# Nyström attention and a multiplicative feed-forward on one Trainium2 core: the landmark product on GpSimd, the norm chain as a stage of its own, and the stages interleaved from a written list

## The chip, the cores and the metric

The kernel runs on one core of a Trainium2 chip. The metric is device time in microseconds; lower is better. A core has five engines that run side by side, each taking its own instructions in program order: TensorE (PE in the profile; its weight loads are PEld), VectorE (DVE), ScalarE (ACT), GpSimd (POOL) and SyncE (SP), which here only issues transfers. Matmuls write PSUM; VectorE and ScalarE read it.

## The reference, cut to what matters

Each of 8 batch items ("images" below) has 8 heads of 576 rows of 64 numbers. Attention goes through 32 landmarks, means of 18 rows each. The result of all heads, 4608 rows of 512, goes through the feed-forward.

```python
q_lm = q.reshape(B, H, m, S // m, D).mean(axis=3)      # m = 32
k_lm = k.reshape(B, H, m, S // m, D).mean(axis=3)
A  = softmax(q @ k_lm.T / 8)       # 576 x 32
Bm = softmax(q_lm @ k_lm.T / 8)    # 32 x 32
C  = softmax(q_lm @ k.T / 8)       # 32 x 576
Z = Bm.T / (norm1(Bm) * norminf(Bm) + 1e-06)
for _ in range(6):
    Z = 2 * Z - Z @ Bm @ Z
attn = A @ Z @ C @ v
h = (x @ w1) * (x @ w2) @ w3       # x: attn, heads side by side
out = h @ w_out
```

## The kernel before, in words

**Preparation.** `fold` multiplies w3 by w_out once into one matrix `w34`, while the first transfers arrive (L497 to L500). It is a generator: each `steps(fd, n)` lets it emit n more products, and the attention of image 0 is emitted between them. Loads of q and k go through POOL's queue (`qk_pieces`, L93), transposes of them, v and the output through SP's (L106, L85, L467).

**Per image.** `sums` (POOL, L176 to L181) adds rows towards the landmarks, `landmarks` finishes them with a copy on ACT (`far`, L195) and an addition on POOL (L196), into `qbd` and `lm`. Then `attention(st)`, also a generator, emits the small attention products in 13 stages, each ended by `yield`:

1. C0: scores of half the heads against all keys (L211), exponential on ACT into `ect` (L215), partial sums on POOL (`presum`, L222 to L227).
2. B: the landmark scores (L238), `ebm` on ACT (L242), row sums and reciprocal on DVE (`rbs`, L245, L246), the product `bm` on DVE (L248), its 32x32 transpose `bt` (L251), and `btm` on POOL (L253).
3. C1 (the other half of the heads), its presum, then the norm chain on DVE: column sums `cs`, transpose `csT`, maximum, scaling and reciprocal into `nrn` (L261 to L268); `bmn` and `bmbd` on POOL (L270, L273).
4. R: bt times btm (L300), from which DVE makes `sz_` and `tz_`, two operations for each half (L306, L308); then A0 and A1 (L285, exponentials at L291), and cv, C times v (L317), with reciprocal and scaling on DVE (L325, L326).
5. to 10. the six iterations (L376; L381, L383), with denominators (L337), their reciprocals in three parts (L346), and in the last one the first `normalise` (L361, L364).
11. Z (L398), `zt`, the second `normalise`.
12. and 13. G: zt times w1 and w2 (L419), copied to `gt` by ACT (L423) and DVE (L425).

**The main loop** goes over images b. It emits for image b the `up` products (L433): for j in 0 to 7 the half u (w1), copied by ACT to `a_sb` (L437), and the half v (w2), multiplied with a_sb by DVE into `ab` (L439). Then come the `down` products (L451), in halves of four matmuls, 8 halves for an even image and 10 for an odd one, evicted by ACT (L460). Between these it emits the stages of the attention of image b+1, at fixed places: stages 1 to 4 after u1, u2, u4 and u6, stage 5 after v7, and then one stage after each half of down. Here too stand the preparations for image b+2: `sums` after v5, `landmarks` and the four pieces of v. The last image has no attention beside it.

**What sets the order.** The schedule is manual: each engine executes in the order in which the code emits. PSUM has three buffers named `big`, shared by C, A, up, the iterations, normalise, G and part of down; one `acc` (B, R, the second cv, down) and one `small`. A matmul that takes a buffer waits until the engine that reads its last content has done so.

Of the kernel before, what the change touches and what calls it, by code (L numbers as in the profile page):

```python
# [7 lines left out]
FP32 = mybir.dt.float32  # L8
FP16 = mybir.dt.float16
AXF = mybir.ActivationFunctionType  # L10
ALU = mybir.AluOpType
AX = mybir.AxisListType

B = 8
# [17 lines left out]
def kernel(  # L32
# [20 lines left out]
    def big():  # L53
        return psp.tile([128, 2, 512], FP32, name="big", bufs=3)
# [145 lines left out]
    def attention(st, bank=None):  # L200
# [35 lines left out]
        for qd in range(2):  # L236
            for h in range(4):
# [7 lines left out]
        nc.vector.reduce_sum(out=rbs, in_=ebm, axis=AX.X)  # L245
        nc.vector.reciprocal(out=rbs, in_=rbs)  # L246
        bm = pz.tile([128, 2, 32], FP32, name="bm")
        nc.vector.tensor_tensor(out=bm, in0=ebm,  # L248
                                in1=rbs.unsqueeze(2).to_broadcast([128, 2, 32]), op=ALU.mult)
        bt = pz.tile([128, 2, 32], FP32, name="bt")  # L250
        nc.vector.transpose(out=bt, in_=bm)  # L251
        btm = pz.tile([128, 2, 2, 32], FP32, name="btm")
        nc.gpsimd.tensor_tensor(  # L253
            out=btm, in0=bt.unsqueeze(2).to_broadcast([128, 2, 2, 32]),
            in1=par32.unsqueeze(1).unsqueeze(3).to_broadcast([128, 2, 2, 32]), op=ALU.mult)
        yield

        scores_c(1)
        es1 = presum(1)
        cs = pz.tile([128, 2], FP32, name="cs")  # L260
        nc.vector.reduce_sum(out=cs, in_=bt, axis=AX.X)  # L261
        csT = pz.tile([128, 2, 32], FP32, name="csT")
        nc.vector.transpose(out=csT, in_=cs.unsqueeze(2).to_broadcast([128, 2, 32]))
        nrn = pz.tile([128, 2], FP32, name="nrn")
# [28 lines left out]
            eat.append(e)  # L293

        side = acc if bank is acc else (lambda: big()[:, 0, :])
        psR = side()
        for qd in range(2):
            for h in range(4):
# [3 lines left out]
                                 tile_position=(64 * (h // 2), 32 * h))  # L302
        sz_ = pz.tile([128, 2, 96], FP32, name="sz_")
        tz_ = pz.tile([128, 2, 32], FP32, name="tz_")
        for qd in range(2):
            nc.vector.tensor_scalar(out=sz_[:, qd, 0:32], in0=psR[:, 32 * qd:32 * qd + 32],  # L306
                                    scalar1=nrn[:, qd:qd + 1], scalar2=None, op0=ALU.mult)
            nc.vector.scalar_tensor_tensor(  # L308
                out=tz_[:, qd, :], in0=psR[:, 32 * qd:32 * qd + 32], scalar=nrn[:, qd:qd + 1],
                in1=eye2[:, qd, :], op0=ALU.mult, op1=ALU.add)  # L310
        scores_a(0)
        scores_a(1)

        def cv(qd, es, psV):
            for r in range(6):
                for h in range(4):
                    nc.tensor.matmul(  # L317
                        psV[32 * h:32 * h + 32, 0:64], ects[qd][0:NP, h, r, :],
                        vt[0:NP, 4 * qd + h, 64 * r:64 * r + 64],
                        start=(r == 0), stop=(r == 5), tile_position=(0, 32 * h))  # L320
            for h in range(4):
                nc.tensor.matmul(psV[32 * h:32 * h + 32, 64:65], es[0:NP, h, :], ones[0:NP, :],
                                 start=True, stop=True, tile_position=(0, 32 * h))
            rcr = pz.tile([128, 1], FP32, name="rcr")
            nc.vector.reciprocal(out=rcr, in_=psV[:, 64:65])  # L325
            nc.vector.tensor_scalar(out=sz_[:, qd, 32:96], in0=psV[:, 0:64],  # L326
                                    scalar1=rcr[:, 0:1], scalar2=None, op0=ALU.mult)

        psX = small()
        cv(0, es0, psX)  # L330
# [197 lines left out]
    def steps(g, n=1):  # L528
        for _ in range(n):
            next(g, None)  # L530
# [3 lines left out]
    with tc.tile_pool(name="pf", bufs=2) as pf:  # L534
        wof, w3f = {}, {}
        wsp = pf.tile([128, 2, 8, DM], FP16, name="wsp", bufs=1)

        def load_w3(j, cc=None, eng=nc.sync):
            if j not in w3f:
                w3f[j] = pf.tile([128, DF], FP32, name="w3f", bufs=3)  # L540
            sl = slice(0, DF) if cc is None else slice(512 * cc, 512 * cc + 512)
            eng.dma_start(out=w3f[j][:, sl], in_=moe_w3[128 * j:128 * (j + 1), sl])

        def load_wout(c, eng):
            wof[c] = pf.tile([128, DM], FP32, name="wof", bufs=6)
            eng.dma_start(out=wof[c], in_=moe_w_out[128 * c:128 * c + 128, :])

        load_w3(0, 0)
        load_wout(0, nc.scalar)
        load_wout(1, nc.sync)  # L550
        load_w3(1, 0, nc.scalar)
        load_wout(2, nc.sync)
        load_wout(3, nc.scalar)
        load_w3(0, 1)
        load_wout(4, nc.scalar)
        load_w3(1, 1)
        load_wout(5, nc.scalar)

        warm = pf.tile([128, 512], FP16, name="warm", bufs=1)
        nc.vector.memset(warm, 0.0)  # L560
        psw = big()

        def warm_up(n):
            for _ in range(n):
                nc.tensor.matmul(psw[:, 0, :], warm[:, 0:128], warm, start=True, stop=True)

        warm_up(7)

        nc.gpsimd.tensor_copy(out=gate, in_=wof[4][:, 0:1])
        load_qk(sts[0], 0)  # L570
        load_qk(sts[1], 1)
        load_weight(0, moe_w1)
        load_weight(1, moe_w2)
        par32, mask4, ones, eye2, onesq, selc, lomask = constants()
        fd = fold(pf, wof, w3f, wsp, warm_up)
        steps(fd, 1)
        load_wout(6, nc.sync)
        load_wout(7, nc.sync)
        load_w3(2)
        steps(fd, 7)  # L580
        load_w3(3)
        steps(fd, 8)
        w3f[4] = pf.tile([128, DF], FP32, name="w3f", bufs=3)
        nc.gpsimd.tensor_copy(out=w3f[4][0:NP, 0:1], in_=sts[0]["qkn"][0:NP, 0, 0, 0:1])
        load_w3(4)
        sts[0]["vt"] = pin.tile([128, H, 384], FP32, name="vt")
        nc.gpsimd.tensor_copy(out=sts[0]["vt"][0:NP, 0, 0:1], in_=sts[0]["qkn"][0:NP, 1, 0, 0:1])
        load_v(sts[0], 0)
        turn_on_pe(sts[0], 0, 0, nc.scalar.copy)
        turn_on_pe(sts[0], 0, 4, nc.vector.tensor_copy)  # L590
        sums(sts[0], 0)
        steps(fd, 5)
        turn_on_pe(sts[0], 1, 0, nc.scalar.copy)
        turn_on_pe(sts[0], 1, 4, nc.vector.tensor_copy)
        load_w3(5)
        steps(fd, 2)
        landmarks(sts[0], 0, 0)
        landmarks(sts[0], 0, 1)
        sums(sts[0], 1)
        steps(fd, 2)  # L600
        load_w3(6)
        turn_all(1)
        steps(fd, 5)
        at = attention(sts[0])
        for n, m in enumerate((2, 2, 3, 3, 2, 1, 1, 1, 1, 2, 2, 3, 3)):
            steps(at)
            if n == 0:
                load_w3(7)
            elif n == 3:
                pieces = qk_pieces(sts[2], 2)  # L610
                sums(sts[1], 0, pieces=pieces)
                sums(sts[1], 1, pieces=pieces)
            if 2 < n < 7:
                load_v_piece(sts[1], 1, n - 3, ident[0:NP, 0:1])
            elif n > 10:
                landmarks(sts[1], 0, n - 11)
            steps(fd, m)
            if n == 0:
                landmarks(sts[0], 1, 0)
                landmarks(sts[0], 1, 1)  # L620
                steps(fd, 2)
        steps(at, 30)
        landmarks(sts[1], 1, 0)
        steps(fd, 64)
    pab = ctx.enter_context(tc.tile_pool(name="pab", bufs=2))
    at = attention(sts[1], acc)


    for b in range(B):
        st = sts[b]  # L630
        if b % 2 == 0:
            ab = pab.tile([128, 8, 2 * S], FP16, name="ab")
        st["ab"], st["t0"] = ab, S * (b % 2)
        if b + 2 < B:
            turn_all(b + 2)
        chunks = range(0, 512, 128) if b % 2 == 0 else range(512, 2 * S, 128)
        for j in range(8):
            up(st, j, 0)
            if b + 1 < B and j == 0:
                landmarks(sts[b + 1], 1, 1)  # L640
            steps(at, (0, 1, 1, 0, 1, 0, 1, 0)[j])
            if b + 2 < B and j > 5:
                load_v_piece(sts[b + 2], b + 2, j - 6, ident[0:NP, 0:1])
            up(st, j, 1)
            if b + 2 < B and j == 5:
                pieces = qk_pieces(sts[b + 3], b + 3) if b + 3 < B else iter(())
                sums(sts[b + 2], 0, pieces=pieces)
                sums(sts[b + 2], 1, pieces=pieces)
        steps(at, 1)
        hold = {}  # L650
        nd = 2 * len(chunks)
        for n in range(nd):
            bank = (lambda: big()[:, 0, :]) if n // 2 % 2 else acc
            down(ab, b - b % 2, chunks[n // 2], n % 2, hold, bank)
            if b + 2 < B and n in (1, 3):
                load_v_piece(sts[b + 2], b + 2, 2 + n // 2, ident[0:NP, 0:1])
            steps(at)
            if b + 2 < B and n in (3, 4, 6):
                landmarks(sts[b + 2], n // 6, (n == 4) + 0)
        steps(at, 30)  # L660
        if b + 2 < B:
            at = attention(sts[b + 2], acc)
# [30 lines left out]
```

## Time and profile before

| | |
|---|---|
| runs | 280.36 to 283.4 us, median 282.5 us of 5 |
| the profiled execution | 284.0 us, of which 282.2 us from first to last instruction (the span) |
| `up` L433 on PE | 512 matmuls of 128x288 |
| `ab` L439 on DVE | 64, 47.4 us, mean 749 ns |
| `a_sb` L437 on ACT | 64, 40.9 us, mean 639 ns |
| R work on DVE, one image: L306, L308 | 4 operations of about 245 ns |
| `bmn` L270 on POOL, 128x64 | 8, mean 291 ns |
| DMA | 45.57 MB, mean 161 GB/s |

A row gives an engine's work on a line; the mean is that of one instruction, and instructions that overlap in an engine's pipeline stand closer than their means. The granted clock of PE is full throughout.

### The profile page before, as it was taken

How to read it: one execution, taken by the hardware profiler on the slowest of the kernel's cores; microseconds unless marked ns; L12 is line 12 of the kernel's file. 1: busy time of each engine (PE TensorE's matmuls, PEld its weight loads, DVE VectorE, ACT ScalarE, POOL GpSimd, SP SyncE). 2: the span in 40 equal slices, each digit the busy share in tenths (PEclk: the TensorE clock that was granted, in tenths of full speed). 3: DMA queues.
4: the chain of work that ended last, by engine and by line, in shares of the span. 5: the costliest groups of instructions: out<-in, count | busy, mean ns of one | idle time of the engine just before them, and what ended most of it. 6: DMA issues, size and time to landing. Idle time of an engine off the chain costs nothing.

```text
span 282.2 us, 9481 instructions
## 1 busy us (share of the span) xinstructions
PE 265.7 (94%) x3964; PEld 148.1 (52%) x3964; DVE 164.4 (58%) x439; ACT 137.2 (49%) x259; POOL 162.4 (58%) x210
## 2 busy tenths in 40 slices
PE   7999879899999999999999989999999999999993
PEld 3456435344674466447645654566467446734741
DVE  7734134555287576655765756577568755766610
ACT  3644444026461675357537624664386266615531
POOL 1716863297269948964896599259956954400000
PEclk9999999999999999999999999999999999999999
DMA  6999999999906995899699939995999452014024
GB/s 220 313 234 245 213 251 170 153 253 154 167 5 136 240 219 109 138 281 144 137 174 260 177 90 210 203 169 122 218 197 154 125 161 74 2 39 107 9 74 112
DMA packets 61978, 45.57 MB, mean 161 GB/s; under 512 B 35568, under 2 KB 54000, under 8 KB 61936
## 3 DMA queue, kind: packets, MB, share of 16 engines
q1 hardware_dynamic: 47280, 31.93, 49.8%
q0 software_dynamic: 13824, 11.54, 28.5%
q10 hardware_dynamic: 832, 1.51, 1.6%
q8 instruction: 31, 0.51, 0.8%
q14 instruction: 11, 0.09, 0.1%
HBM read 38.80 MB, written 9.44 MB: 171 GB/s over the span
## 4 chain that ended last, share of the span: by engine, by line
PE 67%; DVE 11%; DMA 8%; ACT 7%; issue 4%; ACTq 0%; POOL 0%; SPq 0%; DVEq 0%; POOLq 0%
PE acc L451 13%; PE big L433 13%; PE big L451 11%; DMA w3f<-in_moe_w_dram 8%; PE acc L497 8%; DVE ab L439 6%; PE big L376 6%; PE big L419 4%; PE small L317 2%; PE big L361 2%; PE small L497 2%; ACT a_sb L437 2%; PE acc L317 2%; ACT gt L423 2%; PE big L484 1%
## 5 line engine op out<-in xcount | busy, mean ns | idle before, releaser
L433 PE MATMUL big<-ahat,gt 128*128 128x288 f16 x512 | 73.0, 286 | 3.5 <-ACT a_sb L437 1.7
L439 DVE TENSOR_TENSOR ab<-a_sb,big 128x576 f16<-128x576 f16 x64 | 47.4, 749 | 24.9 <-ACT a_sb L437 15.8
L433 PEld LDWEIGHTS <-gt 128*128 128x128 f16 x512 | 48.4, 98 | 22.6 <-issue 10.2
L437 ACT CAST a_sb<-big 128x576 f16<-128x576 f32 x64 | 40.9, 639 | 32.4 <-PE big L433 32.3
L497 PE MATMUL acc<-wsp,w3t 128*128 128x512 f16 x168 | 41.1, 379 | 2.2 <-ACT w L500 2.0
L451 PE MATMUL acc<-w,ab 128*128 128x512 f16 x160 | 40.3, 381 | 0.0
L451 PEld LDWEIGHTS <-ab 128*128 128x128 f16 x288 | 24.0, 98 | 29.0 <-issue 4.2
L451 PE MATMUL big<-w,ab 128*128 128x512 f16 x128 | 32.7, 381 | 0.0
L176 POOL TENSOR_TENSOR tr<-qkT 128x768 f32<-128x768 f16 x16 | 26.3, 1643 | 10.0 <-DMA qkT<-qkn 9.8
L460 ACT ACTIVATE o_sb<-acc 128x512 f32<-128x512 f32 (+1 forms) x20 | 11.7, 586 | 37.4 <-PE acc L451 35.8
L497 PEld LDWEIGHTS <-w3t 128*128 128x128 f16 x192 | 17.8, 98 | 21.8 <-issue 3.8
L425 DVE TENSOR_SCALAR gt<-big 128x1024 f16<-128x1024 f32 x16 | 19.6, 1225 | 13.6 <-PE big L419 13.6
L222 POOL TENSOR_TENSOR t<-ect 96x384 f32<-96x384 f32 x16 | 15.9, 995 | 20.2 <-ACT ect L215 17.2
L196 POOL TENSOR_TENSOR lm<-o,far 64x256 f16<-64x256 f32 x16 | 11.6, 724 | 27.3 <-ACT far L195 27.0
L177 POOL TENSOR_TENSOR tr<-tr,qkT 128x768 f32<-128x768 f32 x16 | 26.3, 1643 | 1.3
L490 DVE SCALAR_TENSOR_TENSOR w3t<-big,w3t 128x512 f16<-128x512 f32 x16 | 11.0, 691 | 20.7 <-ACT w3t L489 20.7
L423 ACT ACTIVATE gt<-big 128x1024 f16<-128x1024 f32 x16 | 16.4, 1024 | 13.1 <-PE big L419 13.1
L460 ACT ACTIVATE o_sb<-big 128x512 f32<-128x512 f32 x16 | 9.6, 597 | 16.2 <-PE big L451 16.2
L419 PE MATMUL big<-wup,zt 64*32 64x512 f16 x512 | 17.0, 380 | 0.0
L489 ACT ACTIVATE w3t<-big 128x512 f16<-128x512 f32 x16 | 9.5, 595 | 14.2 <-PE big L484 14.0
L215 ACT ACTIVATE ect<-big 96x768 f32<-96x768 f32 x16 | 12.9, 808 | 2.3 <-PE big L211 2.3
L195 ACT COPY far<-o 64x256 f32<-64x256 f32 x32 | 12.9, 404 | 1.9 <-POOL o L181 1.1
(315 smaller groups left out, 372.2 us busy)
## 6 DMA issues: line engine op xcount, KB each, us to landing
vt<-in_v_dram SPq DMA_DIRECT2D x28, 288.0 KB, 4.2
out_dram<-o_sb SPq DMA_DIRECT2D x23, 192.0 KB, 4.0
qkn<-in_q_dram POOLq DMA_DIRECT2D x12, 288.0 KB, 6.2
qkn<-in_k_dram POOLq DMA_DIRECT2D x12, 288.0 KB, 7.1
w3f<-in_moe_w_dram SPq DMA_DIRECT2D x6, 512.0 KB, 7.9
out_dram<-o_sb SPq DMA_DIRECT2D x24, 128.0 KB, 4.0
wup<-in_moe_w_dram POOLq DMA_DIRECT2D x4, 512.0 KB, 34.1
out_dram<-o_sb SPq DMA_DIRECT2D x24, 64.0 KB, 3.7
```

Source lines behind the costliest of these rows:

```text
L176: nc.gpsimd.tensor_tensor(out=tr, in0=x[:, :, 0, :], in1=x[:, :, 1, :], op=ALU.add)
L177: nc.gpsimd.tensor_tensor(out=tr, in0=tr, in1=x[:, :, 2, :], op=ALU.add)
L376: nc.tensor.matmul(psI[32 * t:32 * t + 32, qd, o:96], tz_[sl, qd, :], sz_[sl, qd, o:96], start=True, stop=True, tile_position=(32 * h, 32 ...
L419: nc.tensor.matmul(psG[32 * h:32 * h + 32, qd, :], zt[rs, i, h, :], wup[rs, h, w, fs], start=(i == 0), stop=(i == 1), tile_position=(64 * ...
L423: nc.scalar.activation(out=g[:, :, w, fs], in_=psG, func=AXF.Copy, scale=1.0 / ZS)
L425: nc.vector.tensor_scalar(out=g[:, :, w, fs], in0=psG, scalar1=1.0 / ZS, scalar2=None, op0=ALU.mult)
L433: nc.tensor.matmul(p[:, c, 0:HS], st["g"][:, qd, w, 128 * j:128 * j + 128], st["ahat"][qd][:, c, :], start=(qd == 0), stop=(qd == 1))
L437: nc.scalar.copy(out=st["a_sb"], in_=p[:, :, 0:HS])
L439: nc.vector.tensor_tensor(out=st["ab"][:, j, st["t0"]:st["t0"] + S].rearrange("p (c s) -> p c s", c=2), in0=st["a_sb"], in1=p[:, :, 0:HS], ...
L451: nc.tensor.matmul(pso[:, :], ab[:, j, t0:t0 + 128], w34[:, j, :], start=(j == 0), stop=(j == 7))
L460: nc.scalar.activation(out=o_sb[:, c], in_=pso[:, c], func=AXF.Copy, scale=1.0 / (X64 * X64))
L497: nc.tensor.matmul(psW[j][:, :], turned[j, c // 4][:, a, c % 4, :], wsp[:, b, c, :], start=(c == 0 and a + b == 0), stop=(c == 7 and a == 1))
```

## The change

bm is computed by GpSimd. Its transpose bt, btm and the column sums cs move from stage 2 to stage 3, behind C1's scores and ahead of the presum. The norm chain (csT to bmbd) is a stage of its own, so there are 14 stages. In the stage after it A0 is emitted first, then R; `sz_` for both halves comes from one VectorE operation, `tz_` from GpSimd; the scalings of cv go to ScalarE.

```diff
-        nc.vector.tensor_tensor(out=bm, in0=ebm,
+        nc.gpsimd.tensor_tensor(out=bm, in0=ebm,
                                 in1=rbs.unsqueeze(2).to_broadcast([128, 2, 32]), op=ALU.mult)
+        yield
+
+        scores_c(1)
         bt = pz.tile([128, 2, 32], FP32, name="bt")
         nc.vector.transpose(out=bt, in_=bm)
...
-        yield
-
-        scores_c(1)
-        es1 = presum(1)
         cs = pz.tile([128, 2], FP32, name="cs")
         nc.vector.reduce_sum(out=cs, in_=bt, axis=AX.X)
+        es1 = presum(1)
+        yield
+
         csT = pz.tile([128, 2, 32], FP32, name="csT")
...
+        scores_a(0)
         psR = side()
...
-        for qd in range(2):
-            nc.vector.tensor_scalar(out=sz_[:, qd, 0:32], in0=psR[:, 32 * qd:32 * qd + 32],
-                                    scalar1=nrn[:, qd:qd + 1], scalar2=None, op0=ALU.mult)
-            nc.vector.scalar_tensor_tensor(
-                out=tz_[:, qd, :], in0=psR[:, 32 * qd:32 * qd + 32], scalar=nrn[:, qd:qd + 1],
-                in1=eye2[:, qd, :], op0=ALU.mult, op1=ALU.add)
-        scores_a(0)
+        nc.vector.tensor_tensor(out=sz_[:, :, 0:32],
+                                in0=psR[:, 0:64].rearrange("p (a m) -> p a m", m=32),
+                                in1=nrn.unsqueeze(2).to_broadcast([128, 2, 32]), op=ALU.mult)
+        nc.gpsimd.tensor_tensor(out=tz_, in0=sz_[:, :, 0:32], in1=eye2, op=ALU.add)
         scores_a(1)
...
-            nc.vector.tensor_scalar(out=sz_[:, qd, 32:96], in0=psV[:, 0:64],
-                                    scalar1=rcr[:, 0:1], scalar2=None, op0=ALU.mult)
+            nc.scalar.activation(out=sz_[:, qd, 32:96], in_=psV[:, 0:64], func=AXF.Copy,
+                                 scale=rcr[:, 0:1])
```

Beside the fold, image 0's stages get new distances, and the preparation of image 1 starts one stage later:

```diff
-        for n, m in enumerate((2, 2, 3, 3, 2, 1, 1, 1, 1, 2, 2, 3, 3)):
+        for n, m in enumerate((2, 2, 2, 3, 3, 2, 1, 1, 1, 1, 2, 2, 2, 2)):
...
-            elif n == 3:
+            elif n == 4:
                 pieces = qk_pieces(sts[2], 2)
...
-            if 2 < n < 7:
-                load_v_piece(sts[1], 1, n - 3, ident[0:NP, 0:1])
-            elif n > 10:
-                landmarks(sts[1], 0, n - 11)
+            if 3 < n < 8:
+                load_v_piece(sts[1], 1, n - 4, ident[0:NP, 0:1])
+            elif n > 11:
+                landmarks(sts[1], 0, n - 12)
```

In the main loop the order is now read from a list of names. u and v with a number are halves of up, d is a half of down, a is one attention stage, g, h and k are landmarks, s is sums, p is a piece of v:

```diff
+    UP = "u0 g a v0 u1 a v1 u2 v2 u3 a v3 u4 a v4 u5 a s v5 u6 a p v6 u7 a p v7 "
+    EVEN = "d a d p a h d a h d a p d a d a k d a d"
+    ODD = "d d a d p a h d a h d a p d a d a k d a d d"
...
-        for j in range(8):
-            up(st, j, 0)
-            if b + 1 < B and j == 0:
+        if b < B - 1:
+            names = UP + (EVEN, ODD)[b % 2]
+        else:
+            names = "u0 v0 u1 v1 u2 v2 u3 v3 u4 v4 u5 v5 u6 v6 u7 v7" + 10 * " d"
...
+        for t in names.split():
+            if t[0] in "uv":
+                up(st, int(t[1]), "uv".index(t[0]))
+            elif t == "d":
+                bank = (lambda: big()[:, 0, :]) if n // 2 % 2 else acc
+                down(ab, b - b % 2, chunks[n // 2], n % 2, hold, bank)
+                n += 1
+            elif t == "a":
+                steps(at)
...
-            steps(at, (0, 1, 1, 0, 1, 0, 1, 0)[j])
...
-        steps(at, 1)
...
-        for n in range(nd):
-            bank = (lambda: big()[:, 0, :]) if n // 2 % 2 else acc
-            down(ab, b - b % 2, chunks[n // 2], n % 2, hold, bank)
-            if b + 2 < B and n in (1, 3):
-                load_v_piece(sts[b + 2], b + 2, 2 + n // 2, ident[0:NP, 0:1])
-            steps(at)
-            if b + 2 < B and n in (3, 4, 6):
-                landmarks(sts[b + 2], n // 6, (n == 4) + 0)
```

So stages 1 to 7 follow u0, u1, u3, u4, u5, u6 and u7, and stages 8 to 14 stand between the halves of down: after the first half of an even image, after the second of an odd one. Stage 14, the second G, is followed by one more half in an even image and by two in an odd one.

More of the change, by code (lines that the diff above doesn't have):

```diff
@@ L636 @@
         chunks = range(0, 512, 128) if b % 2 == 0 else range(512, 2 * S, 128)
-        for j in range(8):
-            up(st, j, 0)
-            if b + 1 < B and j == 0:
-                landmarks(sts[b + 1], 1, 1)
-            steps(at, (0, 1, 1, 0, 1, 0, 1, 0)[j])
[L642 to L645, printed above, removed]
-                pieces = qk_pieces(sts[b + 3], b + 3) if b + 3 < B else iter(())
-                sums(sts[b + 2], 0, pieces=pieces)
-                sums(sts[b + 2], 1, pieces=pieces)
@@ L649 @@
-        steps(at, 1)
-        hold = {}
-        nd = 2 * len(chunks)
-        for n in range(nd):
-            bank = (lambda: big()[:, 0, :]) if n // 2 % 2 else acc
-            down(ab, b - b % 2, chunks[n // 2], n % 2, hold, bank)
-            if b + 2 < B and n in (1, 3):
-                load_v_piece(sts[b + 2], b + 2, 2 + n // 2, ident[0:NP, 0:1])
-            steps(at)
-            if b + 2 < B and n in (3, 4, 6):
-                landmarks(sts[b + 2], n // 6, (n == 4) + 0)
+        if b < B - 1:
+            names = UP + (EVEN, ODD)[b % 2]
+        else:
+            names = "u0 v0 u1 v1 u2 v2 u3 v3 u4 v4 u5 v5 u6 v6 u7 v7" + 10 * " d"
@@ new lines @@
+        soon = sts[b + 2] if b + 2 < B else None
+        hold, n, parts, halves = {}, 0, 0, 0
+        for t in names.split():
[7 more added lines that the diff above has]
+                steps(at)
+            elif t == "g":
+                landmarks(sts[b + 1], 1, 1)
+            elif soon is not None and t == "s":
+                pieces = qk_pieces(sts[b + 3], b + 3) if b + 3 < B else iter(())
+                sums(soon, 0, pieces=pieces)
+                sums(soon, 1, pieces=pieces)
+            elif soon is not None and t == "p":
+                load_v_piece(soon, b + 2, parts, ident[0:NP, 0:1])
+                parts += 1
+            elif soon is not None and t == "h":
+                landmarks(soon, 0, halves)
+                halves += 1
+            elif soon is not None and t == "k":
+                landmarks(soon, 1, 0)
```

## The prediction

> **What bounds the kernel now.** I read the page's busy shares first, then the slices for the TensorE (PE) clock, then the chain of waits.
>
> ```profile
> PE 265.7 (94%) x3964; PEld 148.1 (52%) x3964; DVE 164.4 (58%) x439; ACT 137.2 (49%) x259; POOL 162.4 (58%) x210
> PEclk9999999999999999999999999999999999999999
> PE 67%; DVE 11%; DMA 8%; ACT 7%; issue 4%; ACTq 0%; POOL 0%; SPq 0%; DVEq 0%; POOLq 0%
> ```
>
> PE is busy 94% at full clock. But the chain is PE for only 67%, so about a third of the end is set by something else. The 8% DMA (w3f, until 42.5 us) and 4% issue don't depend on the changed lines; the 11% VectorE (DVE) and 7% ScalarE (ACT) do. To see where, I printed PE's timeline over one image, b=2 (start, length, columns as in the page, idle in brackets).
>
> ```profile
> 126.98 1.63 PE L433 MATMUL big<-ahat,gt 128*128 128x288 f16 x12
> 128.50 0.70 PE L211 MATMUL big<-qbd,qkT 128*96 128x64 f16 x12
> ...
> 132.30 0.65 PE L433 MATMUL big<-ahat,gt 128*128 128x288 f16 x4 [0.24 <-ACT a_sb L437]
> 132.89 0.68 PE L211 MATMUL big<-qbd,qkT 128*96 128x64 f16 x12
> 133.56 2.38 PE L433 MATMUL big<-ahat,gt 128*128 128x288 f16 x16
> ...
> 151.42 1.07 PE L419 MATMUL big<-wup,zt 64*32 64x512 f16 x32
> 152.43 2.04 PE L433 MATMUL big<-ahat,gt 128*128 128x288 f16 x12
> ```
>
> Here 12 `up` matmuls flow in 1.63 us at the head of image 2 (in the chain, 1.47), but the 12 that follow L419 directly at 152.43 take 2.04: **0.41 us lost at the head of an odd image**. And 16 take 2.38 where 4/3 of 1.47 is 1.96. The chain over the same stretch says who holds PE:
>
> ```profile
> 130.91 0.24 ACT ebm L242
> 131.15 0.02 issue
> 131.17 0.23 DVE rbs L245
> ...
> 131.69 0.24 DVE bm L248
> 131.93 0.02 issue
> 131.95 0.17 DVE bt L251
> 132.13 1.38 DVE ab L439 x2
> 133.50 0.13 DVE cs L261
> ...
> 152.17 0.98 ACT gt L423
> ```
>
> Small norm operations stand on DVE in front of the `ab` products that free PE's `big` buffers, and at the image's end PE's second `up` (v0) waits for the 0.98 us gt copy. From 126.98 to the first `down` (140.19) the up stretch takes 13.2 us. Its pieces, free of waits: 16 ups at 0.49, C 2 x 0.58, B 0.15, R and A 0.55, cv 1.58, first iteration 0.35, denominators 0.24: 11.9. So **about 1.3 us per image is waiting**, and the down stretch is dense (halves of 4 at 0.97 or 0.86, nothing idle).
>
> **What the Trainium skill says.** "Perfetto Trace Analysis", section Identifying the Most-Contended Engine: matmul busy share is no measure of distance to the limit. The trace agrees: an L433 row lasts 286 ns, yet 12 pass in 1.47 us, 122 ns each. "PSUM — Partial Sum Buffer", section Engine vs sequencer instructions: ScalarE, VectorE and GpSimd queues are strict FIFO; the chain above agrees, ab behind bt. "GPSIMD Engine Reference", section 4.1: GpSimd cannot read PSUM, and is about 2x slower for two inputs. Here L270 (POOL, 128x64) takes 291 ns against 241 for DVE's L248: 1.2x. "SBUF — State Buffer", section Who interferes with whom: a DVE instruction with two SBUF inputs blocks, or is blocked by, a GpSimd one. bm on DVE was such a one and goes away; no row shows that contention, so I take 0.
>
> **The change, part by part.**
>
> *DVE, ACT and POOL work.* DVE loses bm (241 ns), 3 of 4 R operations (the four span 136.27 to 137.0, 0.73; one stays at about 0.25, so 0.48) and two cv scalings (2 x 0.28): about 1.3 us per image. ACT gains two copies of 128x64 from PSUM; nearest rows 229 ns (ebm L242) and 272 (L403), I take 0.25 each. POOL gains bm and tz at 0.29 each (L270). Neither engine is full (49%, 58%), so the cost is only where PE waits for them.
>
> *Stages move up.* C0 now follows u0 (it followed u1), R and A follow u5 (not u6), and iterations 0 and 1 run between ups, so iteration 1 leaves the down stretch (0.35 us, same work on PE) and the last G (L419) of every even image gets a `down` behind it.
>
> I placed all engines by hand from u0 at 0, with these durations, 0.15-0.2 us from a PE end to ACT or DVE, 0.06 back, and the buffers that the built order shows. As a test, the old order placed so puts R at 8.64; the trace has 135.94 - 127.14 = 8.8. New order, times in us:
> - C0 to 1.07, v0 1.56, u1 2.05, B 2.2. ACT: the previous o_sb 0.58, a_sb 1.24, far 1.66, ect0 2.46. **v1 needs ect0's buffer: wait 0.35.** Before, u1 and v1 covered this.
> - ebm 3.0 to 3.23 (behind the next a_sb), rbs and its reciprocal to 3.6, then ab1 to 4.35. **u3 waits for ab1: 0.4.**
> - POOL: g's lm to 2.4, presum0 (2.03 long) to 4.55, bm to 4.85. DVE reaches bt at about 5.0: bm is in time by 0.15. btm, presum1, bmn, bmbd to 9.7, tz to 10.0; iteration 0 comes at 11.0: hidden by 1.0.
> - The norm chain (0.8) runs at 6.9 to 7.7, ab4 to 8.4. A1 takes u5's buffer, and u5 ends only 0.4 (A0, R) before: **wait 0.4.**
> - cv to 10.0, v5, u6, iteration 0 at 11.0: ACT's two copies end by 10.7, hidden by v5 and u6 (two ups, 1.0 us). **v7 waits for ab6: 0.1-0.2.**
> - v7 ends at 13.5. Like for like the old order needs 13.2 + 0.35 = 13.55.
>
> So the waits change place and hardly size: 0 per image, bounds -0.6 (all that the lighter DVE could give) and +0.4, times 7 images: **0, -4.2 to +2.8**. The first image runs beside the fold: there, the final gt, far and the w copy L500 hold PE 0.56 us before 68.45; in the new order L500 is queued ahead of gt: **-0.5** (0 to -0.8, or +0.3 if its new w boundary waits as the 0.25 at 48.02 did).
>
> *The tail.* After an even image's G1, d7's 0.86-0.97 us covers gt's 0.98-1.22. I take the 0.41 at all four odd heads (images 1, 3, 5, 7; rows at 99.00, 152.43 and 206.67 read 2.04): **-1.6** (-1.9 if measured to the first down, image 3's 167.02 - 152.43 less 0.91 of issue being 13.68 against 13.2; 0 if o_sb, queued behind gt, takes its place).
>
> *Moved at no cost.* landmarks' h comes two halves earlier: o of the first sums is ready at about 15.5 (sums start behind tz at 10.0; before, 10.5), far is asked at 16.2. If late, ACT stands still, but its next o_sb has 4 us. POOL's qkn loads follow sums and keep their time; SP's out stores and vt loads stay in the same order, and the vt pieces p have most of an image before cv. No load gets nearer its use by more than 1 us.
>
> Sum: 0 - 0.5 - 1.6 = **-2.1 us**. The profiled execution took 284.0 (span 282.2): it becomes 281.9. It lies 1.5 above the median 282.5, which becomes **280.4**.
>
> **The rivals.** (1) *Buffers come free earlier.* DVE 1.3 us lighter in a stretch where the chain shows it, so 0.6 of the 1.3 us of waits goes: 7 x -0.6 - 2.1 = -6.3, **276.2**. For it: DVE is the largest non-PE part of the chain. Against: my placing finds three new waits, two not on DVE. (2) *POOL becomes the bound, slower.* bm stands behind g's lm and presum0 on a strict FIFO; bt waits for it, and behind bt stand cs, ab3, the norm chain and ab4. From bm ending at about 5.9 instead of 4.85, ab3 (wanted at 6.15) is pushed one for one. At 0.8 us per image beyond that: 7 x 0.8 - 2.1 = +3.5, **286.0**. For it: margin only 1.0 after 2.8 us of POOL queue; against: POOL idled 0.7 and 1.85 us there before. (3) *Nothing gained*: the new waits are 0.3 larger, 7 x 0.3 = 2.1, **282.5**. The change is done as its words say (counts below), so no rival there.
>
> **How the numbers follow.** Chances: forecast 0.40 (own range 278.5 to 282.5), (1) 0.28, (2) 0.22, (3) 0.10. 1% is 2.8 us: below 279.7 is faster, above 285.3 slower, about what this kernel's measurement tells from no change. A third of the forecast's range is below 279.7: faster 0.14 + 0.28 = 0.42; same 0.26 + 0.10 = 0.36; slower 0.22. Range: 276.0 to 285.0, leaving out the outer parts of (1) and (2), each about 0.1.
>
> **What would show it.** DVE 391 instructions (439 - 8 bm - 24 R - 16 cv) and about 152 us, ACT 275 (259 + 16), POOL 226 (210 + 8 bm + 8 tz). The head of odd images: no 12 at 2.04 behind L419. New PE idle named ect at v1, ab at u3, a_sb at L285's second group. u0 to v7's end 13.5 us: 12.9 means (1). POOL in the chain, or bt waiting over 0.5 for bm, means (2). I am wrong if iteration 0 waits for tz, or if down stretches get gaps.

## The result, and the profile after

The changed kernel takes **283.0 us** (median of 36 runs, 281.7 to 287.9), the kernel before 281.2 (median of 71, among them the five of the table). The ratio is **1.0086, 95% interval 1.0066 to 1.0106**: slower by 0.9%, 2.4 us. The ratio is of executions in the fast state alone, while the medians also hold slower ones, so it isn't the quotient of the two. The forecast was 2.1 us in the other direction.

The first profile of the kernel before had a disturbed start: the first up matmul of image 0 stood at 73.62 us, and at 69.93 and 70.19 in the two profiles taken of it since, while the stretches of the images agree within 0.1 us. So the comparison below uses these two (spans 278.3 and 278.5) and two of the changed kernel (280.6 and 280.7).

The page of the changed kernel, busy shares and PE clock first, then the chain of waits by engine:

```profile
PE 263.2 (94%) x3964; PEld 148.8 (53%) x3964; DVE 153.7 (55%) x391; ACT 142.4 (51%) x275; POOL 166.7 (59%) x226
PEclk9999999999999999999999999999999999999999
PE 74%; ACT 9%; DVE 8%; issue 4%; DMA 1%; POOL 1%; ACTq 0%; DVEq 0%
```

DVE is 11 us lighter with the forecast 391 instructions, ACT has 275, POOL 226. The POOL share of the chain is 1%: POOL is not the bound. All that was to be moved was moved, and the time went up.

PE's timeline over the up stretch of image 2 in the changed kernel (start, length, line, tiles, tile size, shape, count, idle time before the row with its releaser):

```profile
125.01 0.65 PE L433 MATMUL big<-ahat,gt 128*128 128x288 f16 x4
125.50 0.69 PE L211 MATMUL big<-qbd,qkT 128*96 128x64 f16 x12
126.03 1.15 PE L433 MATMUL big<-ahat,gt 128*128 128x288 f16 x8
127.10 0.22 PE L238 MATMUL acc<-lm,qbd 64*32 64x32 f16 x8
127.70 2.40 PE L433 MATMUL big<-ahat,gt 128*128 128x288 f16 x16 [0.38 <-ACT ect L215]
129.94 0.69 PE L211 MATMUL big<-qbd,qkT 128*96 128x64 f16 x12
...
132.65 0.32 PE L287 MATMUL big<-qkT,lm 64*32 64x288 f16 x8
132.78 0.31 PE L303 MATMUL acc<-bt,btm 64*32 64x32 f32 x16
133.45 0.32 PE L287 MATMUL big<-qkT,lm 64*32 64x288 f16 x8 [0.36 <-ACT a_sb L437]
133.69 0.88 PE L317 MATMUL small<-vt,ect 96*32 96x64 f32 x48
...
138.50 0.65 PE L433 MATMUL big<-ahat,gt 128*128 128x288 f16 x4
138.99 1.03 PE L451 MATMUL acc<-w,ab 128*128 128x512 f16 x4
```

v1 waits 0.38 us for `ect`, A1 (the second L287 row) 0.36 for `a_sb`. The same view of the kernel before from C1 to the R stage, where R and both A groups follow u6 and nothing waits in that stage; its rows are short because the profile splits interleaved matmuls:

```profile
129.24 0.68 PE L211 MATMUL big<-qbd,qkT 128*96 128x64 f16 x12
...
132.22 0.25 PE L300 MATMUL acc<-bt,btm 64*32 64x32 f32 x6
...
132.36 0.52 PE L285 MATMUL big<-qkT,lm 64*32 64x288 f16 x12
132.81 0.88 PE L317 MATMUL small<-vt,ect 96*32 96x64 f32 x48
```

From the stage's first row to cv it took 132.81 - 132.22 = 0.59 there, and takes 133.69 - 132.65 = 1.04 now. The chain of the changed kernel runs through u3 and through this place:

```profile
128.75 0.66 DVE ab L439
129.41 0.04 issue
129.45 0.65 PE big L433 x4
...
132.76 0.65 ACT a_sb L437
133.41 0.04 issue
133.45 0.32 PE big L287 x8
```

A1's PSUM buffer is the one that u5 has just filled: the wait ends with ACT's copy out of it, which takes 0.65 us. Only A0 and R stand between u5 and A1. In the kernel before A1 takes the buffer of v5, with u6 (0.49 us) between.

The table splits each span: the head of image 0 (first up matmul), images 0, 2, 4, 6 from head to next head, images 1, 3, 5 likewise plus image 7's up stretch, all without the pauses on PE that the timeline puts down to issue, then these pauses from image 0 on ("issue" is idle time in which PE waits for nothing that the profile shows). The last 13.7 us, image 7's down and the end, are equal in all kernels.

| us | head of image 0 | even images | odd images | pauses | span |
|---|---|---|---|---|---|
| before, two profiles | 69.93, 70.19 | 101.87, 101.86 | 91.67, 91.66 | 1.17, 1.08 | 278.3, 278.5 |
| after, two profiles | 70.32, 70.03 | 103.23, 103.23 | 91.42, 91.43 | 1.96, 2.31 | 280.6, 280.7 |
| difference of the means | +0.1 | **+1.4** | -0.2 | **+1.0** | +2.25 |

### The profile page after: what moved, and what is told of

It is laid out like the page before. It is cut to its first block, busy times and chain, and to the rows that moved or that the text cites. A ratio compares the mean times of both kernels' runs of the same rounds, so it can differ in the third digit from the quotient of the medians.

```text
span 280.6 us, 9477 instructions
## 1 busy us (share of the span) xinstructions
PE 263.2 (94%) x3964; PEld 148.8 (53%) x3964; DVE 153.7 (55%) x391; ACT 142.4 (51%) x275; POOL 166.7 (59%) x226
## 4 chain that ended last, share of the span: by engine, by line
PE 74%; ACT 9%; DVE 8%; issue 4%; DMA 1%; POOL 1%; ACTq 0%; DVEq 0%
PE big L433 13%; PE acc L451 13%; PE acc L497 11%; PE big L451 11%; PE big L419 6%; DVE ab L439 5%; PE big L376 4%; ACT a_sb L437 4%; PE big L211 2%; PE small L317 2%; ACT ect L215 2%; PE big L361 2%; PE big L484 2%; PE small L497 2%; PE acc L317 2%
## 5 line engine op out<-in xcount | busy, mean ns | idle before, releaser
L439 DVE TENSOR_TENSOR ab<-a_sb,big 128x576 f16<-128x576 f16 x64 | 48.0, 750 | 26.9 <-PE big L433 12.7
L451 PEld LDWEIGHTS <-ab 128*128 128x128 f16 x288 | 24.8, 98 | 29.9 <-issue 5.9
L451 PE MATMUL acc<-w,ab 128*128 128x512 f16 x160 | 39.7, 380 | 0.0
L425 DVE TENSOR_SCALAR gt<-big 128x1024 f16<-128x1024 f32 x16 | 19.6, 1225 | 13.2 <-PE big L419 13.2
```

Source lines behind the costliest of these rows:

```text
L425: nc.vector.tensor_scalar(out=g[:, :, w, fs], in0=psG, scalar1=1.0 / ZS, scalar2=None, op0=ALU.mult)
L439: nc.vector.tensor_tensor(out=st["ab"][:, j, st["t0"]:st["t0"] + S].rearrange("p (c s) -> p c s", c=2), in0=st["a_sb"], in1=p[:, :, 0:HS], ...
L451: nc.tensor.matmul(pso[:, :], ab[:, j, t0:t0 + 128], w34[:, j, :], start=(j == 0), stop=(j == 7))
```

## The experiments

Theories: **order** (the new places of the stages cost, since a buffer's reader gets less cover), **engines** (the moved operations cost, on POOL or ACT), **start** (the loss lies beside the fold).

**The kernel before again.**

> The kernel before, unchanged, for a second profile and for the spread. Its first profile took 284.0 us, 2.8 above the median of the many runs, and 18.6 us of its chain was one w3f transfer. If that start was disturbed (theory 'start'), image 0's first up stands near 71 us here instead of 73.6, the span is near 278.5, and all stretches from image to image are as in the first profile within 0.1 us. If it was not, the start is again at 73.6 and the difference lies in the images. Ratio 1.000.

281.2 us, ratio 0.9994 (0.9968 to 1.002), span 278.3: the clean base of the table.

**The engines moved, stages and places old.** The kernel before with only these lines of the diff: bm on GpSimd, `sz_` in one operation, `tz_` on GpSimd, the scalings of cv on ScalarE. Lines of this kernel from the R stage on have numbers smaller by two.

> The kernel before with the engine moves alone (bm and tz on GpSimd, R's sz in one VectorE operation, cv's scaling on ScalarE), stages and order as before. Theory 'order' (the new places of the stages cost the time, the moves do not): up stretch of an image 13.2 us or up to 0.5 less, total 0 to 3 us less than before, ratio 0.990 to 1.000. Theory 'engines' (bm behind presum on GpSimd, sz by way of ScalarE hold PE up): up stretch 0.4 longer, total 2 to 3 us more, ratio 1.007 to 1.010.

359.3 us, ratio **1.282** (1.273 to 1.290), outside both expected ranges. POOL's timeline in image 0's up stretch:

```profile
90.68 1.65 POOL L176 TENSOR_TENSOR tr<-qkT 128x768 f32<-128x768 f16 x1
...
95.40 0.80 POOL L181 TENSOR_TENSOR o<-o,tr 128x256 f32<-128x256 f32 x1
96.14 0.69 POOL L93 DMA_DIRECT2D qkn<-in_k_dram  x1
96.84 0.33 POOL L308 TENSOR_TENSOR tz__1233<-sz__1232,eye 128x64 f32<-128x64 f32 x1
```

And PE in the same stretch:

```profile
97.23 0.57 PE L374 MATMUL big<-sz__1232,tz__1233 32*32 32x96 f32 x16 [10.68 <-POOL tz__1233 L308]
```

At the old places `sums` is emitted after v5 and the R stage after u6, so the 0.33 us `tz_` stands behind all eight operations of `sums` in POOL's queue, and iteration 0 waits 10.68 us. This is the strict FIFO that "PSUM — Partial Sum Buffer", section Engine vs sequencer instructions, states. The change avoids it: it puts the R stage ahead of `s`. So this run doesn't measure the moved operations; one below does.

**The changed kernel's order, old engines.** bm, `sz_`, `tz_` and the scalings go back to VectorE.

> The changed kernel with bm, R and cv's scalings back on VectorE as before, the new stages and order kept. Theory 'order': as slow as the changed kernel or slower, ratio to before 1.008 to 1.015, up stretch to v7's end 14 us or more. Theory 'engines': the loss is gone, ratio 0.993 to 1.002, up stretch 13.5.

283.7 us, ratio 1.0103 (1.0055 to 1.0151), against 1.0086 for the whole change. The new stages and places with the old engines are as slow as the whole, as the order theory had it; the intervals leave some 2 us open. PE's timeline in image 2, where the granted clock is full (L435 is `up`):

```profile
126.16 0.65 PE L435 MATMUL big<-ahat,gt 128*128 128x288 f16 x4
...
128.84 1.63 PE L435 MATMUL big<-ahat,gt 128*128 128x288 f16 x12 [0.38 <-ACT ect L215]
...
131.20 0.69 PE L211 MATMUL big<-qbd,qkT 128*96 128x64 f16 x12
...
133.91 0.32 PE L287 MATMUL big<-qkT,lm 64*32 64x288 f16 x8
...
134.70 0.32 PE L287 MATMUL big<-qkT,lm 64*32 64x288 f16 x8 [0.36 <-ACT a_sb L439]
```

Both waits stand here as in the changed kernel, so no moved operation makes them. The up stretch takes 14.08 us (13.98 with the moves), and 14.04 and 14.09 in images 0 and 4 (13.93 and 13.98): the moves are worth 0.1 us an image, and it is won ahead of C1 (5.04 here, 4.93 with the moves). From C1 to A0 both take 2.71.

**Stages later.** The changed kernel with its stages back near the old places, `sums` where it was:

```diff
-    UP = "u0 g a v0 u1 a v1 u2 v2 u3 a v3 u4 a v4 u5 a s v5 u6 a p v6 u7 a p v7 "
+    UP = "u0 g v0 u1 a v1 u2 a v2 u3 v3 u4 a v4 u5 a v5 s u6 a p v6 u7 a p v7 a "
```

> The changed kernel with stages 1 to 7 each about half an up pair later: C0 after u1, B after u2, C1 after u4, the norm chain after u5, R and A after u6, iteration 0 after u7, iteration 1 after v7; down as in the changed kernel. Theory 'order' in its narrow form (v1 waits for ect0, u3 for ab1, A1 for u5's a_sb): these three waits of about 0.4 each go, iteration 1 waits about 0.25 for sz, so some 0.5 us less per image than the changed kernel, 3 to 4 us in all, ratio to before 0.993 to 0.998. If the waits only move again: ratio as the changed kernel, 1.006 to 1.010.

356.6 us, ratio 1.269 (1.263 to 1.275): `s` stands ahead of the R stage and so of `tz_` again, the same trap (iteration 0 waits 11.05 us). A1's wait of 0.36 is there all the same; of the total it tells nothing about the order.

**The engines moved, old places, `sums` behind the R stage.** As the second experiment, `sums` emitted after u6's stage. The profiled execution of the first run took 1382 us, so the stretches below are from a second one.

> moves_old_order with the sums of image b+2 behind stage 4 instead of ahead of it, so that tz_ no longer stands behind some 11 us of sums in GpSimd's queue. If that place alone made it 78 us slower, the loss is gone. Then theory 'order' expects the engine moves to be harmless: up stretch of an even image 12.7 to 13.2 (before 13.15 to 13.21), ratio to before 0.988 to 1.000. Theory 'engines' expects 13.5 or more, ratio 1.006 to 1.010.

> The same kernel as in the run before of this name (engines moved, old stages, old places, sums behind the R stage), whose profiled execution was useless for reading stretches. 1.02 again. If the later sums make a landmark or a first iteration wait, its image stretches of even images are longer by 0.5 to 1 us than 13.2 + 12.2, with POOL named; if the moved operations themselves cost, R, cv or the first iteration show DVE or ACT waits in up and down is 12.2.

287.2 and 285.2 us, ratios 1.021 (1.0145 to 1.027) and **1.018** (1.013 to 1.024). The chain in image 1 of the second:

```profile
130.94 1.00 POOL t L222
...
132.54 0.45 POOL es L227
132.99 0.26 POOL bm L248
...
133.28 0.04 DVE bt L251
...
133.44 1.38 DVE ab L437 x2
```

bm stands behind presum's operations on POOL; `bt`, left at its old place, waits on DVE, and two `ab` products stand behind it. The first matmul of C1 pays, as the timeline of PE shows:

```profile
134.21 0.68 PE L211 MATMUL big<-qbd,qkT 128*96 128x64 f16 x12 [0.62 <-DVE ab L437]
```

(0.68 in the next image.) Even images take 104.74 in the table's column, +2.9. So bm on GpSimd with `bt` where it was costs some 0.7 us an image ((104.74 + 93.70 - 101.87 - 91.67) / 7), most of it in this wait. In the changed kernel, where `bt` comes behind C1's scores, the wait isn't there; the move of `bt` was not tried alone. Its head of image 0 is 3.0 us later as well; 1.74 of that is a pause that no run here explains.

**The new stages at the old places, `sums` behind `tz_`.** One stage after each half of down again:

```diff
+    UP = "u0 g v0 u1 a v1 u2 a v2 u3 v3 u4 a v4 u5 a v5 u6 a s p v6 u7 p v7 a "
+    EVEN = "d a d p a h d a h d a p d a d a k d a d a"
+    ODD = "d a d a d p a h d a h d a p d a d a k d a d d"
```

> The changed kernel's 14 stages and its engines at the old places: C0 after u1, B after u2, C1 after u4, the norm chain after u5, the R stage after u6, iteration 0 after v7, one stage after each half of down, sums behind the R stage so that tz does not stand behind them. Order theory: the new places alone cost the 0.30 us of an even image and alone give the cover at odd heads, so both go and it stands where the kernel before stands, 0.997 to 1.003, with 12 ups at about 2.0 behind the last G at odd heads again. If instead the split of the norm chain, or A0 ahead of R, costs: 1.005 to 1.010.

280.7 us, ratio **1.0002** (0.9977 to 1.0028). The time is what the order theory had, but not the way to it. PE's timeline:

```profile
133.58 0.32 PE L287 MATMUL big<-qkT,lm 64*32 64x288 f16 x8 [0.36 <-ACT a_sb L437]
...
148.83 1.07 PE L419 MATMUL big<-wup,zt 64*32 64x512 f16 x32
149.84 2.04 PE L433 MATMUL big<-ahat,gt 128*128 128x288 f16 x12
```

The 12 ups in 2.04 behind the last G are back, so the new places do remove that loss. A1's 0.36 is there too: it comes with the new stages, whatever their place, where the expectation laid the loss to the places alone. Which of the stages' edits hands A1 a fresher buffer was not tried alone. Even images take 102.45, +0.6 over the kernel before, the odd ones 91.80, +0.1, the pauses are 0.67. (The head of image 0 stands at 71.10 in this one profile, 1.0 later, which the ratio over 22 runs doesn't show.) So the new stages pay for most of A1's wait by gains ahead of it; C1 and the four halves of up behind it take 2.71 us here too, and took 132.22 - 129.24 = 2.98. The new places add 0.8 in even images, take 0.4 off odd ones, and have pauses 1.3 to 1.6 longer.

**A1 behind the first half of cv.** If A1's wait is the loss, putting 0.8 us of other matmuls ahead of it removes it:

```diff
-        scores_a(1)
...
         cv(0, es0, psX)
+        scores_a(1)
         cv(1, es1, side())
```

> The changed kernel with A1 emitted between the two halves of cv, so that its wait for u5's buffer (0.36 us before A1 in the changed profile) is filled by cv0. Theory 'order': up stretch of an even image 13.6 instead of 13.98, 7 x 0.36 = 2.5 us less, ratio to before 0.998 to 1.001. If the wait only moves (to iteration 0, by way of the later eat or sz on ScalarE): 13.95, ratio 1.006 to 1.010.

280.1 us, ratio **0.9984** (0.9958 to 1.001), span 278.2. PE's timeline in image 2:

```profile
131.58 0.31 PE L303 MATMUL acc<-bt,btm 64*32 64x32 f32 x16
131.82 0.88 PE L316 MATMUL small<-vt,ect 96*32 96x64 f32 x48
132.52 0.22 PE L321 MATMUL small<-ones,es 96*32 96x1 f32 x8
132.66 0.32 PE L287 MATMUL big<-qkT,lm 64*32 64x288 f16 x8
```

No wait at L287. Even images 101.83 (-1.4 against the changed kernel), odd 90.51 (-0.9), pauses 1.84, head 70.37: 2.3 us in seven images, some 0.33 in each: as much as the whole loss.

**Iteration 1 behind v7**, without and with the edit to A1 (`u7 a p v7` becomes `u7 p v7 a`):

> The changed kernel with iteration 1 behind v7 instead of between u7 and v7. v7 then takes iteration 0's buffer and no longer waits for ab6, which stands on VectorE behind the first reciprocal (0.33 us of waiting before v7). Theory 'order': up stretch with iteration 1 13.65 instead of 13.98, 7 x 0.33 = 2.3 us less, ratio 0.999 to 1.002. If iteration 2, now half a down nearer, waits for sz instead: 13.98 in the sum, ratio 1.006 to 1.010.

> Both of the two edits. If the two waits are the cost of the new order and independent: 4.8 us less than the changed kernel, 277.5 us, ratio to before 0.990 to 0.994, faster than before. If both waits stood in front of the same later wait: no more than the better of the two, 0.998 to 1.001.

285.0 us, ratio 1.0174 (1.0136 to 1.0212), outside both expected ranges, and 280.5 us, 0.9995 (0.9965 to 1.003), which is the second of its expectations: no more than the edit to A1 gives. The wait ahead of v7 is 0.16 in the changed kernel, not 0.33: the expectation counted iteration 1's own 0.33 as waiting (138.50 - 138.01 - 0.33). The up stretch of image 2 is shorter by about that, 13.83 for 13.98, but the next iteration now waits:

```profile
140.09 0.40 PE L376 MATMUL big<-sz__2499,tz__2497 32*32 32x96 f32 x16 [0.21 <-DVE sz__2499 L383]
```

Only one half of down stands between iterations 1 and 2, and DVE has v7's `ab` to do first. The wait changed its place. That does not account for all of the 1.0174; the pauses, 2.83 in this profile, are larger as well, and the rest is open.

**C0 one half later**, with A1 behind the first cv: `u0 g a v0` becomes `u0 g v0 a`; in the second run B too (`u1 a v1 u2` becomes `u1 v1 a u2`).

> The same with C0 alone one half later, B and all others where the change puts them. Order theory: v1's wait for ect goes, u3's stays; half to all of the gain of the run with both, ratio 0.988 to 0.996. If the chain from B to the norm sets the time (ebm behind ect on ScalarE, with C0 now nearer to B): v2 or u3 waits longer for what v1 no longer waits, ratio 0.998 to 1.003.

> The changed kernel with A1 behind cv of the first half, and besides C0 one half later (behind v0) and B one half later (behind v1), all other stages where the change puts them. Order theory (a stage's first matmul, or the up half behind it, takes a PSUM buffer whose reader has had only one half of up, about 0.5 us, to be done): the 0.38 at v1 behind C0 gets u1 as cover, and the wait of u3 gets one more half too; 0.3 to 0.4 us per image for seven images on top of what A1 gave, so 277 to 278.5 us, ratio 0.985 to 0.993. If C0 itself then waits for the first a_sb, or the wait is only handed on (as it was when iteration 1 was moved): no gain on A1 alone, ratio 0.997 to 1.001.

278.9 us, ratio **0.9925** (0.9898 to 0.9952), and 278.8 us, **0.9915** (0.9878 to 0.9952). PE's timeline of the first:

```profile
124.87 0.69 PE L211 MATMUL big<-qbd,qkT 128*96 128x64 f16 x12
125.39 0.65 PE L433 MATMUL big<-ahat,gt 128*128 128x288 f16 x4
125.98 0.22 PE L238 MATMUL acc<-lm,qbd 64*32 64x32 f16 x8
126.13 1.65 PE L433 MATMUL big<-ahat,gt 128*128 128x288 f16 x12
128.01 0.65 PE L433 MATMUL big<-ahat,gt 128*128 128x288 f16 x4 [0.24 <-ACT a_sb L437]
```

v1's 0.38 is gone; u1 covers `ect` again. The 0.24 is u3's; in the changed kernel u3 waits 0.28 for `ab`, so this wait is not new. The even images fall to 100.99 and the odd to 89.67, another 0.8 each, 0.24 for each of seven images. Moving B removes u3's 0.24 and gives no difference that these intervals tell (even images 100.45). Both beat the kernel before.

**Second and third profiles.**

> The changed kernel once more, unchanged, for a second profile. If the issue pauses and the start belong to the change: pauses of about 1.2 in image 1 and 0.75 in image 3 again, and image 0's head again 0.3 to 0.5 behind that of the kernel before. If they belong to the execution: they differ by as much as the two kernels did. The image stretches come again within 0.05 us in both cases: even images 13.9 to 14.0 and 11.75. Time 283.0, ratio 1.006 to 1.011.

> The kernel before, unchanged, for a third profile. If the issue pauses and the start belong to the order: pauses of 0.5 in image 1 and 0.65 in image 3, head of image 0 at 69.9. If they belong to the execution: others. Stretches of even images 13.2 and 12.2.

282.7 us for the changed kernel, ratio 1.009 (1.0057 to 1.0122); 280.3 us in the one run of the kernel before. They are the second numbers in the table. The stretches repeat within 0.02 us in sum. The pauses do not cross (1.1, 1.2 and, in the first profile, 1.4 before; 2.0 and 2.3 after), so on these five profiles they go with the order. The heads of image 0 do cross, so the start is equal within what two profiles tell; in the experiments with the new start it stands between 70.03 and 71.24.

## Why the prediction was wrong

The failing step is the sum of the up stretch, "So the waits change place and hardly size: 0 per image". Measured: up 13.98 against 13.21 in image 2 (iteration 1, 0.33, is new in it), down 11.76 against 12.23, so **+0.30 net in an even image, +1.4 over four**. It lies inside the bound of +0.4; the value taken was wrong. The 0 came from setting a stretch placed by hand, 13.5, against a measured one, 13.2 + 0.35. The placing's own test had put R of the old order 0.16 too early (8.64 for 8.8), and it put v7's end of the new order 0.48 too early. So a loss of 0.3 lay within what the placing could not tell.

- *The single waits were sized about rightly.* v1 0.35 for `ect`: 0.38. u3 0.4 for `ab`: 0.28 (129.45 in the chain, less 127.70 and three halves of 0.49). A1 0.4 for u5's `a_sb`: 0.36. v7 0.1 to 0.2: 0.16. The prediction's own times (cv to 10.0, less 1.58, 0.4 of waiting and 0.55) put the R stage at about 7.5 after the head: 132.65 - 125.01 = 7.64. bm was in time by 0.15: 0.13. By the prediction's own pieces free of waits (11.87, and 0.33 for iteration 1) the new stretch loses 1.8 us, and the four waits are 1.2 of it. The other 0.6 is spread over rows without a named wait, such as two halves of up in 1.09 instead of 0.98, twice.
- *The gain ahead of them was not the lighter DVE's.* 7.64 is 0.27 ahead of the old order, once its two more halves of up (0.98) are taken off 132.22 - 123.33 = 8.89. All of it lies between C1 and R (2.71 for 2.98), and it is there with the old engines as well, so the new stages made it; by which edit was not tried. The DVE's 1.3 us less work gave 0.1.
- *What the new waits replace was taken as equal to them.* That 0.27 had to pay for A1's 0.45 (0.59 became 1.04), and after that the placing slipped: cv ended at 10.26 for 10.0 (7.64 + 1.04 + 1.58 gives it), iteration 0 came at 11.35 for 11.0 since two halves of up took 1.09 and not 1.0, and v7 ended at 13.98 for 13.5. Three small slips in one direction are 0.48 of the stretch; the down stretch then was 0.14 shorter than the loss of iteration 1 explains, which the prediction didn't have. The runs show two terms of this size, A1's wait (0.33 an image, as much as the whole loss, undone by taking it away) and v1's (0.24 an image, won by moving C0 on top of that; not tried alone). The change lost because what was to pay for the waits, the lighter DVE, the tail and the start, gave less than they took.
- *The tail: the right mechanism, smaller.* The 2.04 at odd heads is gone with the new places and back with the old ones. Image 7, which has no attention beside it, shows the gain alone: 8.51 for 8.87, 0.36. If the other three odd images carry the 0.34 of the even ones too, the four heads give -0.24 - 3 x 0.34 = -1.3, where -1.6 was forecast.
- *The start: -0.5 forecast, +0.1 measured.* The 0.56 at L500 before image 0 did go, but in the new order two iterations of image 0's attention wait 0.23 each for `sz` beside the fold (one waited 0.17 before), and a boundary at L500 at 29 us waits 0.67 and 0.48 (two profiles) instead of 0.25, ahead of any stage that changed its place.
- *The pauses: a term put at nothing.* The prediction read one of 0.91 and took it as independent of the change. They grew by 1.0; in image 1 the pause is 0.52 and 0.30 in the old order and 1.21 and 1.15 in the new one. Why is open.
- *The rivals.* (1), buffers free earlier by a lighter DVE, gave 0.1 an image and not 0.6. (2), POOL as the bound, is not what happened: PE waits for none of bm, `bt` and `tz_`, and DVE only once, 0.5 us for bm in image 0 beside the fold. But the run with `bt` at its old place shows the rival's mechanism at some 0.7 us an image. (3), new waits 0.3 larger per image, is the size that came; it stood at "nothing gained" because the tail and the start were to pay for it.

Together: about 2.4 (seven images) + 0.1 - 1.3 + 1.0 = 2.2, the difference of the spans. Of the 4.3 us between forecast and measurement, 2.4 are the up stretch, 1.0 the pauses, 0.6 the start and 0.3 the tail.

## What to carry to other kernels

When work moves between stages, ask of each matmul that takes a buffer which engine read it last and how much PE work stands between that and the taking; a wait that is found must be priced as lost until a measured wait of the same size is shown to go. Compare a placed schedule with the old one placed by the same hand, not with a measured one. Here one score group put behind 0.8 us of other matmuls undid the whole loss, and a stage moved behind one more half of up, on top of that, made the kernel faster than before. A small operation moved to a queue with long ones must be placed ahead of them, not only be short.

## What was not expected of the hardware

- **A pause on PE that no wait explains comes near the same place of its instruction stream.** PE's timeline in image 1, before and after:

```profile
108.39 0.53 PE L433 MATMUL big<-ahat,gt 128*128 128x288 f16 x3 [0.52 <-issue]
```

```profile
108.93 0.36 PE L376 MATMUL big<-sz__1766,tz__1767 32*32 32x96 f32 x6 [1.21 <-issue]
```

The trace's rows ahead of it count 1377 and 1379 matmuls. A second pause comes in image 3, behind 2254 to 2291 matmuls in thirteen profiles. In the old order the first falls among up matmuls (12 in 1.47 us), in the new one among the small ones of iteration 0 (16 in 0.33). That alone doesn't make it long: with A1 behind the first cv it falls on the same iteration and takes 0.58. It took 0.30 to 1.22 in twelve of these profiles, behind 1364 to 1380 matmuls, and is missing in that of the new stages at the old places. What it waits for is not shown, and was not tried.

- **PE's clock after idling.** The clock line of the run with the engines moved at the old places:

```profile
PEclk9999999999579976999589967999599958999998
```

After each wait of some 10 us the granted clock falls to 0.5, and four down matmuls take 1.89 us where they take 1.04 later. "TensorE: Matmul & The Clock Gate", Part 1, says that PE drops to half its clock after an idle window of about 3.4 us; the 10.68 us here agree. The second of the runs with C0 later differs: after a pause of 1.82 us in image 3, about half of that window, its clock was 0.50 from 160 to 162 us and 0.72 from 160 to 165.
